# Sixteen PSUM copies given to ScalarE and four weight tiles converted one place later, in a fused attention and feed-forward kernel

## The chip, the cores and the metric

The kernel runs on one core of a Trainium2 chip. The metric is the time of one execution on the device in microseconds, the median of several runs. The engines are named as in the profile: PE is TensorE's matmuls, PEld its weight loads, DVE is VectorE, ACT is ScalarE, POOL is GpSimd and SP issues the loads.

## What is computed

Causal attention with 2 batches, 12 heads, 448 positions and 64 columns per head gives x of 896 x 768. Then come two feed-forward blocks:

```python
x = attention(q, k, v)                       # 896 x 768
y = ((x @ w1) * (x @ w2)) @ w3 @ w_out       # w1, w2: 768 x 1024; w3: 1024 x 1024; w_out: 1024 x 768
z = np.maximum(y @ w_in2, 0) ** 2 @ w_out2   # w_in2: 768 x 2048; w_out2: 2048 x 768
```

The weights arrive as 8-byte floats, so a tile is loaded as pairs of 32-bit words, and float32 is made of them in the kernel.

## The kernel before

The kernel multiplies w3 by w_out first, while the attention runs, into W (the SBUF tile `wraw`), so that the first block ends in one product with W. This product is cut into 32 **units** (g, i, n): half g of the 1024 inner columns, row tile i of eight, half n of the 768 output columns. A unit is a chain of matmuls into one accumulator of 384 columns (`w_half`, called by `fill`), 12 matmuls in two-part float32 (8 plain float32 ones for the first two row tiles), and one eviction behind it: in the half g = 0 a copy from PSUM into `wraw` (L318), in the half g = 1 an addition onto it (L316). The 16 units with g = 0 come first.

The attention runs over 12 pairs of heads in 13 **slots**. In slot p TensorE computes the scores of pair p, transposes the probabilities of pair p-1 (`p_transposes`, L273), and multiplies them by v (`attend`). In between stand three fills, which place two or three units in a slot from slot 2 on; from slot 4 on the order on TensorE is scores, unit, transposes, units, attend. VectorE takes the row minima of the scores (`minima`, L238), ScalarE the exponentials (`exps`, L245, one call for each head j of a pair) and copies the transposed probabilities out of PSUM (L277), GpSimd divides by the row sums (L255; VectorE does so for a few), and ScalarE and VectorE make the high and the low part of the attended columns (`x_parts`, L119 and L120).

The same two engines convert the weights, in calls of `step`. A step takes one tile from 8-byte words to float32 (the prelu of L102 on ScalarE, L103 and L108 on VectorE) and the tile before it to a high and a low part (the cast of L90 on ScalarE, the subtraction of L106 on VectorE). Which tiles they are follows from the list `order`. A step leaves the float32 part out if two converted tiles still wait for their parts, and leaves the parts out if the buffer is not free; the parts of w3 tile n wait for the units of tile n-2. Each step also issues the loads on SP (L78) of tiles three places ahead.

On TensorE, VectorE and ScalarE the order of this stage is the order in which the code calls the operations (`manual_schedule`, L363). Each engine works through its queue in that order, and an instruction that waits holds up those behind it. So in slot p, from slot 4 on, ScalarE does the exps of head 0, the copies of the transposes, a step, the exps of head 1, further steps and the high part of the attend before; VectorE does the minima, the copy of the first unit, a step, after the exps of head 1 the copies of the other units, further steps and the low part of the attend. Slots 2 and 3 differ in the place of the third unit, which comes behind the attend.

Two pools of PSUM buffers set the waits between the engines. `ps_w` has two: the accumulators of the units and of `attend` take them in turn, so each waits for the eviction of the last but one. Unit (0,1,0) waits for the copy of (0,0,1), unit (0,2,1) for that of (0,2,0), the attend of pair 4 for that of (0,5,0), the attend of pair 5 for that of (0,6,1). `ps_a` has six: the transposes of slot p take the six that the scores of slot p were in, so they wait for the minima of slot p; the next scores wait for ScalarE's copies of these transposes.

After slot 12 the big products follow, x by w1 and w2, by W, by w_in2 and by w_out2, whose order a planner sets.

Of the kernel before, what the change touches and what calls it, by code (L numbers as in the profile page):

```python
# [17 lines left out]
def attention_moe_moe2(ctx: ExitStack, tc: tile.TileContext, qk, v, w1, w2, w3, w_out, w_in2, w_out2, out):  # L18
# [13 lines left out]
    nc = tc.nc  # L32
# [35 lines left out]
    def mm(o, l, r, start, stop):  # L68
        return nc.tensor.matmul(o, l, r, start=start, stop=stop)  # L69
# [61 lines left out]
    NB = W3N // P  # L131
    order = []
    for g in range(N3 // KF):
        for i in range(KF):
            order += [("w3", g * KF + i)]
            if g == 0 and i == 0:
                order += [("wout", f) for f in range(NB)]
            if g == 0 and NB - 1 <= i < 2 * NB - 1:
                order += [("wout", i + 1)]
    order += ring[KF:]  # L140
    source = {"wout": w_out, "w1": w1, "w2": w2, "w3": w3, "win2": w_in2, "wout2": w_out2}
    place = {key: i for i, key in enumerate(order)}
# [36 lines left out]
    with (  # L179
# [121 lines left out]
        def w_half(g, i, n):  # L301

            n3, cols = g * KF + i, slice(n * HN, (n + 1) * HN)
            acc = ps_w.tile([P, HN], F32, tag="w", name=f"w{n3}_{n}")
            for f in range(NB):
                c = slice(f * P, (f + 1) * P)
                if n3 < PLAIN:
                    mm(acc, f32s["w3", n3][:, c], f32s["wout", f][:, cols], f == 0, f == NB - 1)
                    continue
                t, wo = hls["w3", n3], hls["wout", g * NB + f]  # L310
                for s, r in ((0, 0), (0, 1), (1, 0)):
                    mm(acc, t[:, s, c], wo[:, r, cols],
                       f == 0 and (s, r) == (0, 0), f == NB - 1 and (s, r) == (1, 0))
            dst = wraw[:, i, cols]
            if g > 0:
                nc.vector.tensor_tensor(dst, acc, dst, op=ALU.add)  # L316
            else:
                nc.vector.tensor_copy(dst, acc)  # L318

        units = [(g, i, n) for g in range(N3 // KF) for i in range(KF) for n in range(2)]  # L320
        NU = len(units)
# [33 lines left out]
        def fill():  # L355
            done[0] += 1
            n = max(0, done[0] - LEAD) * NU // (GAPS * SLOTS - LEAD) - done[1]
            for _ in range(n):
                w_half(*units.pop(0))
                done[1] += 1  # L360
# [159 lines left out]
    acc = big.tile([P, NTT, DM], F32, tag="W", name="acc")  # L520
# [92 lines left out]
```

## Time and profile before

| | us |
|---|---|
| median of 3 runs | 577.47 |
| lowest and highest run | 577.46, 577.71 |
| the profiled execution | 577.6 |
| its span, from the first to the last instruction | 575.4 |
| PE busy in the span | 563.9 |
| DVE busy | 281.3 |
| ACT busy | 268.2 |
| POOL busy | 159.1 |

A busy time is the sum over an engine's instructions. The chain that ended last is followed back from the last instruction, at each step to what released it. In a timeline the first number is the start in us from the span's start, the second the time from the first start to the last end of a run of equal instructions, and the bracket at the end is the idle time before the row and what ended it. An instruction's end overlaps the start of the next one on the same engine.

### The profile page before, as it was taken

To read this page: it belongs to the slowest core of one execution; us is meant where nothing else is said; L and a number is where in the kernel's file an instruction comes from. 1 tells how busy PE (TensorE), PEld (TensorE's weight loads), DVE (VectorE), ACT (ScalarE), POOL (GpSimd) and SP (SyncE) were. 2 spreads that over 40 slices of the span, in tenths; PEclk is the share of its full clock that TensorE was granted. 3 is DMA by queue.
4 is the path that set the end of the run, shared out by engine and by line. 5 is a ranking of instruction groups with operands and counts; after the bars stand their busy time and mean duration, and the time that the engine had idled before them with its cause. 6 is when DMAs were issued, how large, how long until landed. Compare 5 with 4: busy or idle time off the path is not lost.

```text
span 575.4 us, 8129 instructions
## 1 busy us (share of the span) xinstructions
PE 563.9 (98%) x3144; PEld 506.5 (88%) x3144; DVE 281.3 (49%) x567; ACT 268.2 (47%) x574; POOL 159.1 (28%) x140
## 2 busy tenths in 40 slices
PE   7899999999999999999999999999999999999997
PEld 5557777778989999999999999999999999999997
DVE  5987887767687544222210484555102854421011
ACT  5778777757865533222210456666002666640000
POOL 3367677776200312111100003333000023330000
PEclk9999999999999999999999999999999999999999
DMA  8854554233266633000000274333100763000111
GB/s 318 288 194 140 177 159 159 84 124 120 88 225 245 204 120 107 9 1 1 1 1 0 67 271 156 109 111 110 56 1 4 270 219 110 1 1 29 56 55 56
DMA packets 14823, 63.96 MB, mean 111 GB/s; under 512 B 1665, under 2 KB 1921, under 8 KB 14785
## 3 DMA queue, kind: packets, MB, share of 16 engines
q1 hardware_dynamic: 14784, 63.45, 32.2%
q8 instruction: 25, 0.41, 0.3%
q14 instruction: 14, 0.11, 0.1%
HBM read 60.69 MB, written 2.75 MB: 110 GB/s over the span
## 4 chain that ended last, share of the span: by engine, by line
PE 86%; DVE 6%; ACT 5%; issue 1%; DMA 1%; DVEq 0%; ACTq 0%
PE w L69 28%; PE g L69 20%; PE o L69 20%; PE h L69 10%; PE s L69 3%; PE x L69 2%; PE pp L273 2%; ACT p L245 2%; ACT pt L277 2%; DVE p L238 1%; DVE xw L108 1%; DMA qk<-in_qk 1%; ACT hl_wout L90 1%; DVE raw_wout L103 0%; DVE x_wout L108 0%
## 5 line engine op out<-in xcount | busy, mean ns | idle before, releaser
L69 PE MATMUL g<-hT,hl_win 128*128 128x448 f32 x576 | 117.2, 365 | 0.0
L69 PE MATMUL w<-xT,hl_w 128*128 128x448 f32 x576 | 117.0, 365 | 0.0
L69 PE MATMUL o<-hl_wout,gT 128*128 128x384 f32 x672 | 116.9, 334 | 0.0
L69 PEld LDWEIGHTS o<-hl_wout,gT 128*128 128x128 f32 x672 | 116.6, 188 | 0.1
L69 PEld LDWEIGHTS g<-hT,hl_win 128*128 128x128 f32 x576 | 108.1, 188 | 8.5
L69 PEld LDWEIGHTS w<-xT,hl_w 128*128 128x128 f32 x576 | 108.1, 188 | 8.5
L255 POOL TENSOR_SCALAR p<-p,st 112x448 f32<-112x448 f32 (+1 forms) x84 | 96.5, 1166 | 51.9 <-DVE st L252 23.3
L120 POOL TENSOR_TENSOR gT<-r,gT 128x448 fp32r<-128x448 f32 x32 | 39.1, 1245 | 195.8 <-ACT gT L119 128.7
L69 PE MATMUL w<-hl_wout,w 128*128 128x384 f32 x336 | 64.4, 342 | 0.5 <-DVE w L106 0.3
L245 ACT ACTIVATE p<-p,st 112x448 f32<-112x448 f32 (+1 forms) x96 | 49.7, 530 | 27.1 <-DVE st L238 27.0
L69 PEld LDWEIGHTS w<-hl_wout,w 128*128 128x128 f32 x336 | 57.4, 188 | 3.9 <-issue 0.9
L69 PE MATMUL h<-abT,hl_W 128*128 128x448 f32 x288 | 58.5, 365 | 0.0
L69 PEld LDWEIGHTS h<-abT,hl_W 128*128 128x128 f32 x288 | 54.1, 188 | 4.3
L120 POOL TENSOR_TENSOR abT<-a,abT 128x448 fp32r<-128x448 f32 x16 | 21.8, 1377 | 111.8 <-ACT abT L119 111.8
L238 DVE CUSTOM_DVE_ANT_0 p<-s,mask 112x448 f32<-112x448 f32 (+1 forms) x96 | 36.5, 441 | 7.0 <-PE s L69 7.0
L106 DVE TENSOR_TENSOR hl_wout<-x_wout,hl_wout 128x768 fp32r<-128x768 f32 x20 | 19.1, 957 | 37.9 <-ACT hl_wout L90 37.9
L533 ACT ACTIVATE r<-g 128x448 f32<-128x448 f32 x32 | 15.8, 542 | 40.8 <-PE g L69 40.8
L69 PE MATMUL s<-qk 64*112 64x448 f32 (+3 forms) x192 | 28.6, 443 | 4.1 <-DMA qk<-in_qk 4.1
L560 DVE TENSOR_TENSOR acc<-o,acc 128x384 f32<-128x384 f32 x14 | 7.2, 553 | 49.0 <-PE o L69 49.0
L273 PE MATMUL pp<-ident,p 112*112 112x112 f32 x240 | 27.9, 262 | 3.3 <-DVE st L238 1.6
L102 ACT ACTIVATE x_w<-raw_w 128x768 f32<-128x768 f32 (+1 forms) x30 | 24.4, 815 | 13.7 <-DVE hl_w L106 10.9
L273 PEld LDWEIGHTS pp<-ident,p 112*112 112x112 f32 x240 | 23.5, 134 | 8.0 <-issue 2.8
(62 smaller groups left out, 538.0 us busy)
## 6 DMA issues: line engine op xcount, KB each, us to landing
raw_wout<-in_w_out SPq DMA_DIRECT2D x24, 768.0 KB, 4.5
raw_w<-in_w SPq DMA_DIRECT2D x16, 768.0 KB, 4.3
raw_win<-in_w_in SPq DMA_DIRECT2D x16, 768.0 KB, 4.2
raw_w<-in_w SPq DMA_DIRECT2D x16, 512.0 KB, 3.9
qk<-in_qk SPq DMA_DIRECT2D x12, 448.0 KB, 5.1
v<-in_v SPq DMA_DIRECT2D x12, 224.0 KB, 2.6
out<-acc SPq DMA_DIRECT2D x6, 384.0 KB, 2.3
out<-acc SPq DMA_DIRECT2D x2, 192.0 KB, 1.8
```

The source lines that it names most:

```text
L69: return nc.tensor.matmul(o, l, r, start=start, stop=stop)
L90: nc.scalar.copy(t[:, 0], x)
L102: nc.scalar.activation(y, high.bitcast(F32), AF.Prelu, scale=2.0 ** -112, alpha=-2.0 ** 32)
L106: nc.vector.tensor_tensor(t[:, 1], x, t[:, 0].bitcast(F32), op=ALU.subtract)
L120: (engine or nc.vector).tensor_tensor(lo, x, hi.bitcast(F32), op=ALU.subtract)
L238: nc.vector.tensor_tensor_reduce(e, ps[j, i], mask[:, S - (i + 1) * CP:], QS, 3.0e38, ALU.add, ALU.min, st_t[p][:, 0, j, i:i + 1],)
L245: nc.scalar.activation(e, e, AF.Exp, bias=st_t[p][:, 0, j, i:i + 1], scale=-1.0, accum_out=st_t[p][:, 1, j, i:i + 1])
L255: engine.tensor_scalar(e, e, st[:, 3, i:i + 1], None, ALU.mult)
L273: nc.tensor.transpose(x[:CP, o:o + CP], pt[:, off[i] + c * CP:off[i] + (c + 1) * CP], ident[:CP, :CP],)
L277: nc.scalar.copy(t[:, coff[g[0]]:coff[g[0]] + o], x[:CP, :o])
L533: nc.scalar.activation(r, o[b], AF.Relu)
L560: nc.vector.tensor_tensor(a, o[n], a, op=ALU.add)
```

## The change

In the first half (g = 0) the copy of a unit's accumulator to `wraw` is made by ScalarE and not by VectorE; the call stays at its place in `w_half`, so it lies in ScalarE's queue where it lay in VectorE's. In the list `order`, tiles 4 to 7 of w_out move one place of w3 down: they stood behind w3 tiles 3 to 6, and stand behind w3 tiles 4 to 7.

```diff
             order += [("w3", g * KF + i)]
             if g == 0 and i == 0:
                 order += [("wout", f) for f in range(NB)]
-            if g == 0 and NB - 1 <= i < 2 * NB - 1:
-                order += [("wout", i + 1)]
+            if g == 0 and NB <= i < 2 * NB:
+                order += [("wout", i)]
     order += ring[KF:]
...
             if g > 0:
                 nc.vector.tensor_tensor(dst, acc, dst, op=ALU.add)
             else:
-                nc.vector.tensor_copy(dst, acc)
+                nc.scalar.copy(dst, acc)
```

Here NB is 4 and KF is 8. With the rules of `step` the new order gives these steps where they differ: in slot 2 the loads of w3 4 and w_out 4, and of w3 5 and w_out 5, change places. In slot 3 the second step makes the float32 of w3 4 (it was w_out 4), the last one that of w_out 4 alone (it was w3 4, and the parts of w_out 4). In slot 4 the first step makes the parts of w3 4 alone (it also made the float32 of w_out 5); the parts of w_out 4 to 7 follow in the second step of slot 4, the first and the last of slot 5, and the second of slot 6, and their float32 part comes in the step before each. The first step of slot 7 also makes the float32 of w3 10. Each w3 tile gets its parts in the same step as before.

## Rows read from the trace of the kernel before

**Rows 1.** Windows: PE, PEld, DVE, ACT, POOL busy (count), PEclk, DMA share, GB/s.

```profile
22.00:92.00 70.00, 66.33 (x408) 47.53 (x406) 58.09 (x169) 52.42 (x144) 47.55 (x40) 1.00 0.52 164
92.00:575.00 483.00, 480.07 (x2618) 446.19 (x2616) 208.79 (x349) 199.73 (x387) 102.39 (x87) 1.00 0.27 93
```

**Rows 2.** Timeline of PE: start, us, operation, count, idle before and its releaser.

```profile
33.58 2.85 PE L69 MATMUL w<-xw,w 128*128 128x384 f32 x8 [0.20 <-DVE wraw L318]
...
41.12 2.81 PE L273 MATMUL pp<-ident,p 112*112 112x112 f32 x20
43.70 2.35 PE L69 MATMUL w<-hl_wout,w 128*128 128x384 f32 x12
...
48.31 2.36 PE L69 MATMUL w<-hl_wout,w 128*128 128x384 f32 x12 [0.23 <-DVE wraw L318]
...
54.89 2.08 PE L273 MATMUL pp<-ident,p 112*112 112x112 f32 x20
...
75.04 2.11 PE L69 MATMUL x<-pt,v 112*64 112x448 f32 x16
...
88.03 2.03 PE L69 MATMUL w<-hl_wout,w 128*128 128x384 f32 x10 [0.30 <-DVE w L106]
89.99 2.11 PE L69 MATMUL x<-pt,v 112*64 112x448 f32 x16
...
98.14 2.34 PE L69 MATMUL w<-hl_wout,w 128*128 128x384 f32 x12
...
108.57 4.42 PE L69 MATMUL w<-hl_wout,w 128*128 128x384 f32 x24
...
119.23 2.08 PE L273 MATMUL pp<-ident,p 112*112 112x112 f32 x20
```

**Rows 3.** Groups by line and form: busy us, mean ns | idle before, releasers.

```profile
L318 DVE COPY wraw<-w 128x384 f32<-128x384 f32 x16 | 8.7, 547 | 0.0
...
L556 ACT COPY acc<-o 128x384 f32<-128x384 f32 x7 | 3.4, 479 | 35.3 <-PE o L69 35.3
...
L102 ACT ACTIVATE x_wout<-raw_wout 128x768 f32<-128x768 f32 x20 | 18.3, 917 | 5.6 <-DVE hl_win L106 3.7 <-DMA raw_wout<-in_w_out 1.9
...
L102 ACT ACTIVATE x_w<-raw_w 128x512 f32<-128x512 f32 x14 | 9.7, 695 | 1.4 <-DVE w L106 1.4
```

**Rows 4.** Timeline of ACT; four rows follow directly on exps of head 1.

```profile
33.99 0.83 ACT L90 CAST hl_wout<-xw 128x768 fp32r<-128x768 f32 x1
...
48.60 0.54 ACT L119 CAST xT<-x 128x448 fp32r<-128x448 f32 x1
...
75.37 0.62 ACT L90 CAST w<-x_w 128x512 fp32r<-128x512 f32 x1
...
84.24 2.29 ACT L277 COPY pt<-pp 112x448 f32<-112x448 f32 x6
...
89.55 0.61 ACT L90 CAST w<-x_w 128x512 fp32r<-128x512 f32 x1
```

**Rows 5.** Timeline of DVE: a copy, first minima of slots 5 to 8, what follows.

```profile
32.97 0.55 DVE L318 COPY wraw<-w 128x384 f32<-128x384 f32 x1
...
67.13 0.61 DVE L238 CUSTOM_DVE_ANT_0 p<-s,mask 112x448 f32<-112x448 f32 x1
...
81.52 0.61 DVE L238 CUSTOM_DVE_ANT_0 p<-s,mask 112x448 f32<-112x448 f32 x1
...
94.22 0.62 DVE L238 CUSTOM_DVE_ANT_0 p<-s,mask 112x448 f32<-112x448 f32 x1
...
104.68 0.61 DVE L238 CUSTOM_DVE_ANT_0 p<-s,mask 112x448 f32<-112x448 f32 x1
...
107.63 0.55 DVE L316 TENSOR_TENSOR wraw<-w,wraw 128x384 f32<-128x384 f32 x1
```

**Rows 6.** DMA issues on the page: count, KB each, median us to landing.

```profile
raw_wout<-in_w_out SPq DMA_DIRECT2D x24, 768.0 KB, 4.5
```

**Rows 7.** The chain that ended last, in order of time: start, us, what.

```profile
61.59 0.44 DVE wraw L318
```

## The prediction

> **What bounds the kernel now.** I read the busy windows first, then TensorE's timeline, then what VectorE and ScalarE do just before each gap in it, last the chain that ended last. From 92 us on TensorE lacks 2.93 of 483 us, which is the last tile's way out behind its last matmul; before that it lacks 3.67 of 70 us, though VectorE is busy for 58.1 of them and ScalarE for 52.4 [rows 1]. So whatever TensorE loses or wins before about 110 us moves the end by as much, if nothing before the full stretch gives it back. The granted clock is 1.00 in both windows, 2.4 GHz, so it is no part of the sum.
>
> The gaps are of three kinds [rows 2]. A unit or an attend waits for its ps_w buffer: 0.20 us at 33.58 and 0.23 at 48.31, both released by the copies of L318. The transposes wait for the row minima of their own slot, which free the six ps_a banks: such a group of twenty takes 2.81 us (41.12; three others are alike, at 25.93, 67.90 and 82.29) instead of 2.08 (54.89). A unit waits for the low part of its w3 tile: 0.30 at 88.03. The reader should see that ps_w has two buffers, so that TensorE may be no more than one eviction ahead, and that every one of these waits ends within 0.1 us of what VectorE has just done. The sixteen copies never waited for TensorE: no idle time stands before them [rows 3].
>
> **The copies.** On VectorE each costs 547 ns, on ScalarE a copy of the same 128x384 from PSUM costs 479 [rows 3]. Instructions overlap their successor: six pt copies of 2,240 columns together take 2.29 us from first start to last end (84.24) [rows 4], 0.39 for 384 columns, and the last one's end still overlaps; I put a copy at 0.37 us of queue time. Bounds: nothing, where ScalarE would idle anyway, and 0.48, without overlap. What matters is where it stands in ScalarE's written order: the first unit's copy of a slot comes behind exps(p,0) and ahead of the pt copies, the others behind exps(p,1) and ahead of the conversions. VectorE now copies in parallel with exps(p,1): at 32.97 [rows 5], 0.5 us before that block of exponentials ends (33.99) [rows 4]. On ScalarE the same copy must let the block end first. Queued behind a copy are the pt copies, the conversions, exps(p,1) and the attention casts; TensorE waits for all of them.
>
> **The order of tiles.** Every w3 tile gets its high and low part in the same step as now, tiles 4 to 7 of w_out one step with a free place later. Written out step by step: slot 3's last step makes only the f32 of w_out 4, slot 4's first only the parts of w3 4, slot 6's middle step also the parts of w_out 7, and slot 7's first also the f32 of w3 10; from then on all is as before. An f32 of w_out instead of w3 costs ScalarE 0.22 us more (917 against 695 ns) [rows 3]; dropping one in slot 4 saves 0.8 (its 0.92 less the overlap), the extra one in slot 7 costs 0.57 in the same way. On SP the loads of w_out trade places with those of w3 only, and keep their places among the loads of q, k and v; they stay ahead of their use by over 10 us, against 4.5 us to land [rows 6], and the first user of w_out 4 to 7 is slot 7's second unit, some 5 us behind the last conversion: both at nothing. With that cover gone the unit would wait for one step, about 2 us.
>
> **The sum, slot by slot** (times now, then shifts; a release costs some 0.06 us).
> Slot 2: exps(2,1) ends at 33.99, plus 0.37 for the copy ahead of it, so the copy of unit (0,0,1) ends at 34.36 + 0.48 = 34.84 instead of 33.52, and unit (0,1,0) starts 1.3 us late.
> Slot 3: ScalarE is 0.74 late, VectorE saves a copy of 0.47 on the way to the minima: they come 0.27 late, and transposes paced by them would end at 43.97. TensorE reaches the transposes at 41.12 + 1.3 = 42.4 and is through unstretched at 42.4 + 1.9 = 44.3; unit (0,2,0) starts at 43.70 now, so +0.6 is left. exps(3,1) end at 48.60 + 0.27 + 0.37 - 0.22 = 49.0; copy of (0,2,0) until 49.5; unit (0,2,1) at 49.5 against 48.31: **+1.2**.
> Slot 4: the transposes at 54.89 were not waiting, so the +1.2 stays. ScalarE's pt copies follow the transposes (+1.15), the missing f32 gives 0.8 back, two copies take 0.74, of which VectorE saves 0.44 on the chain [rows 7], and one of them waits about 0.1 for TensorE: minima of slot 5 at +0.75, 67.9 against 67.13 [rows 5].
> Slot 5: eight minima take 2.95 us (104.68 to 107.63) [rows 5] and the last three transposes 0.35 more (three twentieths of 2.08 and a release): the next unit at 71.2, as late as the minima, +0.75. exps(5,1) end at 75.37 + 0.75 + 0.37 = 76.5, the copy of (0,5,0) at 76.97, so attend(4) starts at 77.05 against 75.04: **+2.0**. The way to the minima of slot 6 now runs over ScalarE, late by 1.12 and two copies, and saves VectorE's two copies of 0.44: 82.5 against 81.52.
> Slot 6: the transposes are paced by the minima, +1.0. The cast of w3 7 comes 1.0 + 0.37 later, so does the unit that waited at 88.03: 89.4. exps(6,1) end at 89.55 + 1.0 + 0.37 + 0.22 = 91.2; copy of (0,6,1) 91.65; attend(5) at 91.7 against 89.99: **+1.7**.
> Slot 7: with two copies and w_out 7's parts in one queue (copies to 91.9, cast 92.65, low part 93.6, f32 and low part of w3 8 95.5, f32 of w3 9 and attend's low part) the minima start at 96.65 and their transposes end 3.3 later at 99.95; arriving late, at 98.0 plus 1.9, TensorE says the same. The first unit behind them starts at 98.14 now: **+1.8**.
> Slot 8: from the minima of slot 7 to those of slot 8 ScalarE has a copy (0.37) and the extra f32 (0.57) more, so they start at 104.68 + 2.43 + 0.94 = 108.05, where 2.43 is how late slot 7's are (94.22 now [rows 5]); the last of them and its transposes end at 111.35 against 108.57: **+2.8**.
> Slot 9 on: transposes reach TensorE at 121.9 (119.23 + 2.7), behind minima that start at 119.6; TensorE is the last again and keeps **+2.8 us**.
> From there TensorE is full to the end, so the span goes from 575.4 to 578.2; the profiled execution took 577.6, the median of the runs is 577.47, and I predict 580.3. The copies alone, without the changed order, come to some 2.2 in the same manner, since slots 7 and 8 keep their slack.
>
> **Rivals.** *VectorE's relief wins.* VectorE is the busier engine up to 92 us [rows 1], and four of its copies lie on the chain that ended last with 0.44 to 0.48 us each, one shown [rows 7]. If ScalarE's share fits into its waits for the minima, these 1.8 us are won: 575.7. It decides if the copy of the second unit doesn't hold up TensorE. Against it: those waits come ahead of exps(p,0), the copies behind. The Trainium skill, Perfetto Trace Analysis, Optimizing Scalar/DVE Operations, says that an overloaded DVE may hand work to Scalar, and gives DVE about 125 ns overhead on PSUM against 51 on Scalar. By that rule this rival would be the forecast; the trace agrees on the cheaper copy (479 against 547) and not on what it leads to, since the rule looks at the load and not at the place in the queue.
> *Stretch absorbs it.* Four groups of transposes are stretched by 0.74 us, 3.0 in all [rows 2]; if minima come no later than now, late units only eat that stretch, and not more than 1.1 us is left: 577.5 to 578.6. Against it: the second gap of each pair (48.31, 75.04, 89.99) lies behind the stretch.
> *More is lost.* At 0.48 us of queue time for each of some 13 copies on ScalarE's path, 1.4 us come on top: 581.7. The same happens if GpSimd's division of slot 7, which starts later with exps(7,1), holds up slot 8.
> *The copies move elsewhere in the queue* and cost nothing: the trace of before follows the written order of the three engines in this stage, so I give it no chance of its own.
>
> **How the numbers follow.** Forecast (about +2.8, from 1.2 to 3.6) 0.66, more is lost 0.14, stretch absorbs it 0.12, VectorE's relief 0.08. A measurement of this kernel can tell about 0.2%, 1.15 us, from no change; the third case lies within it, the first two above. Slower 0.80, same 0.12, faster 0.08. The range leaves out, below, relief and nearly all of the third case, and above, the part of the second that is over 582.0: 578.5 to 582.0.
>
> **What would show it.** Right: TensorE's waits at unit (0,1,0), unit (0,2,1), attend(4) and attend(5) are released by ScalarE's copy and last 0.4 to 1.7 us; the minima of slots 7 and 8 start 2 to 4 us later than now; from about 112 us on all is shifted by one amount. Wrong: those waits stay near 0.2 us, or the shift shrinks again behind slot 6, because the copy's place costs less than the end of exps(p,1) says.

## The result and the profile after

The changed kernel takes 581.14 us (median of 5 runs, 581.05 to 581.35) against 577.65 of the kernel before on the same chip: a ratio of 1.0062, 95% interval 1.0048 to 1.0076, so 3.5 us slower (2.8 to 4.4). The span of the profiled execution grew from 575.4 to 578.9 us.

The same two windows as in [rows 1], of the changed kernel (us; busy PE, PEld, DVE, ACT, POOL with counts; PEclk, DMA share, GB/s):

```profile
22.00:92.00 70.00, 63.75 (x392) 46.34 (x390) 46.69 (x147) 55.16 (x153) 46.69 (x38) 1.00 0.45 148
92.00:575.00 483.00, 482.54 (x2630) 447.02 (x2631) 210.25 (x354) 203.46 (x394) 105.27 (x88) 1.00 0.28 95
```

VectorE got what it was to get: 46.69 us busy instead of 58.09. Of the difference some 8 us are the copies; most of the rest is work that now falls behind 92 us. ScalarE took 2.7 us more, and TensorE lacks 6.25 us of this window instead of 3.67. Some 1.2 us more are lost behind it, in slots 7 and 8, where the transposes take 2.34 and 2.82 us and not 2.08.

TensorE's timeline, for [rows 2] (start, us, operation, count, idle before with its releaser):

```profile
34.84 2.85 PE L69 MATMUL w<-xw,w 128*128 128x384 f32 x8 [1.53 <-ACT wraw L318]
...
42.38 2.08 PE L273 MATMUL pp<-ident,p 112*112 112x112 f32 x20
44.23 2.34 PE L69 MATMUL w<-hl_wout,w 128*128 128x384 f32 x12
...
49.40 2.37 PE L69 MATMUL w<-hl_wout,w 128*128 128x384 f32 x12 [0.79 <-ACT wraw L318]
...
77.53 2.11 PE L69 MATMUL x<-pt,v 112*64 112x448 f32 x16 [1.42 <-ACT wraw L318]
...
92.32 2.11 PE L69 MATMUL x<-pt,v 112*64 112x448 f32 x16 [0.48 <-ACT wraw L318]
...
98.66 2.34 PE L273 MATMUL pp<-ident,p 112*112 112x112 f32 x20
100.77 2.35 PE L69 MATMUL w<-hl_wout,w 128*128 128x384 f32 x12
...
109.50 2.82 PE L273 MATMUL pp<-ident,p 112*112 112x112 f32 x20
112.08 4.41 PE L69 MATMUL w<-hl_wout,w 128*128 128x384 f32 x24
...
122.73 2.08 PE L273 MATMUL pp<-ident,p 112*112 112x112 f32 x20
```

Four waits for an accumulator buffer stand there, of 1.53, 0.79, 1.42 and 0.48 us, each released by a ScalarE copy; before, VectorE's copies made it wait 0.20 and 0.23 [rows 2]. The last row starts 3.50 us behind its fellow of before (119.23), and this is what the median lost: nothing behind slot 9 gives any of it back.

Some pieces of the chain that ended last (start, us, what); [rows 7] has one of the four copies of VectorE that stood in it before:

```profile
28.39 0.46 ACT wraw L318
...
34.43 0.36 ACT wraw L318
...
48.98 0.38 ACT wraw L318
...
62.34 0.02 ACT wraw L318
...
77.11 0.75 ACT wraw L318 x2
...
91.90 0.38 ACT wraw L318
```

Before, four copies on VectorE were links of this chain, of 0.44 to 0.48 us each, 1.8 in all. Now ScalarE's copies are links in slots 2, 3, 5 and 6, with 3.4 us in all. In slot 4 the chain runs through TensorE, and the copy has 0.02 us of it.

### The profile page after: what moved, and what is told of

The parts are those of the page before. It is cut to its first block, busy times and chain, and to the rows that moved or that the text cites. A ratio compares the mean times of both kernels' runs of the same rounds, so it can differ in the third digit from the quotient of the medians.

```text
span 578.9 us, 8132 instructions
## 1 busy us (share of the span) xinstructions
PE 564.3 (97%) x3144; PEld 506.2 (87%) x3144; DVE 272.0 (47%) x551; ACT 274.8 (47%) x590; POOL 161.1 (28%) x140
## 4 chain that ended last, share of the span: by engine, by line
PE 86%; ACT 7%; DVE 5%; issue 1%; DMA 1%; DVEq 0%
PE w L69 28%; PE g L69 20%; PE o L69 20%; PE h L69 10%; PE s L69 3%; ACT p L245 3%; PE pp L273 2%; PE x L69 2%; ACT pt L277 1%; DVE p L238 1%; DVE xw L108 1%; ACT hl_wout L90 1%; ACT wraw L318 1%; DMA qk<-in_qk 1%; ACT x_wout L102 0%
## 5 line engine op out<-in xcount | busy, mean ns | idle before, releaser
L255 POOL TENSOR_SCALAR p<-p,st 112x448 f32<-112x448 f32 (+1 forms) x84 | 98.9, 1194 | 53.0 <-DVE st L252 23.8
L69 PE MATMUL s<-qk 64*112 64x112 f32 (+3 forms) x192 | 28.5, 437 | 4.1 <-DMA qk<-in_qk 4.0
```

Source lines behind the costliest of these rows:

```text
L255: engine.tensor_scalar(e, e, st[:, 3, i:i + 1], None, ALU.mult)
```

## The experiments

All times are medians beside runs of the kernel before on the same chip (577.50 us in each of the two series). The edits are shown against the changed kernel, and that of the last run against the kernel before. Two theories run through them. **Place**: a copy costs what its position in ScalarE's queue holds up, TensorE's next accumulator above all. **Load**: each copy costs alike, because ScalarE has more to do.

### The copies alone

```diff
-            if g == 0 and NB <= i < 2 * NB:
-                order += [("wout", i)]
+            if g == 0 and NB - 1 <= i < 2 * NB - 1:
+                order += [("wout", i + 1)]
```

> The sixteen copies are on ScalarE, the order of tiles is that of before. Place (the copies cost by what waits behind them in ScalarE's queue, above all TensorE's four waits for its accumulator buffer): 2.2 us slower than before, 579.8, and unit (0,1,0) starts 1.3 us later than in the kernel before; about 1.3 us of the change's 3.5 are then the order's. Copies are everything: 3.5 us slower, 581.1, and the order costs nothing. VectorE's relief: not slower than before.

Measured: 579.33 us, ratio 1.0035 (1.0022 to 1.0047), by the ratio 2.0 us slower. Unit (0,1,0) waits 1.5 us, as in the full change. From slot 9 on TensorE runs 2.1 us behind the kernel before (scores of slot 9 at 117.06 against 114.96). The copies are the larger part, and VectorE's relief does not outweigh them.

### The order alone

```diff
-                nc.scalar.copy(dst, acc)
+                nc.vector.tensor_copy(dst, acc)
```

> The copies are back on VectorE, the order of tiles is the changed one. Place: TensorE's waits for its accumulator buffers are those of before (0.2 us at units (0,1,0) and (0,2,1)); the f32 of w3 10 in slot 7 and the parts of w_out 7 in slot 6 delay the minima of slots 7 and 8 by 0.5 to 1 us, of which 0.6 us is left: 578.2. The order costs nothing by itself: 577.6, within 0.3 us of before. If the two parts simply add, this run and that of the copies alone give 3.5 us together.

Measured: 577.95 us, ratio 1.0008 (1.0000 to 1.0017), about 0.45 us slower, at the edge of what can be told from no change. That lies between the two expectations. The wait at unit (0,2,1) is gone, which had been expected to stay. The trace shows a gain and a larger loss: attend(5) starts 0.9 us ahead of the kernel before (89.11 against 89.99), then the minima pace the transposes of slots 7 and 8, which take 2.08 us each in the kernel before.

```profile
89.11 2.11 PE L69 MATMUL x<-pt,v 112*64 112x448 f32 x16
...
95.42 2.68 PE L273 MATMUL pp<-ident,p 112*112 112x112 f32 x20
...
106.46 2.55 PE L273 MATMUL pp<-ident,p 112*112 112x112 f32 x20
...
119.44 2.08 PE L273 MATMUL pp<-ident,p 112*112 112x112 f32 x20
```

By slot 9 TensorE is 0.2 us behind (119.44 against 119.23). The two parts give 2.4 us one by one and 3.5 together: they do not add. The same places with the copies alone:

```profile
92.09 2.11 PE L69 MATMUL x<-pt,v 112*64 112x448 f32 x16 [0.21 <-ACT wraw L318]
...
108.82 2.08 PE L273 MATMUL pp<-ident,p 112*112 112x112 f32 x20
...
121.33 2.08 PE L273 MATMUL pp<-ident,p 112*112 112x112 f32 x20
```

Four traces side by side show where the sum fails (start in us; up to 0.2 us of a difference between two traces stands already ahead of slot 2's copies):

| TensorE's work | before | order alone | copies alone | both |
|---|---|---|---|---|
| attend(1), slot 2 | 31.27 | 31.12 | 31.10 | 31.21 |
| attend(5), slot 6 | 89.99 | 89.11 | 92.09 | 92.32 |
| transposes of slot 9 | 119.23 | 119.44 | 121.33 | 122.73 |

From attend(5) to slot 9 the order costs 1.1 us alone (30.33 against 29.24) and 1.2 beside the copies (30.41 against 29.24); the copies cost nothing there. So the later loss adds up, and no slack in slots 7 and 8 is spent twice. What does not add is the order's early gain: from attend(1) to attend(5) it is 0.7 us alone (57.99 against 58.72), and beside the copies it is a loss of 0.1 (61.11 against 60.99). One row of the changed kernel and two of the copies alone show what became of it:

```profile
52.85 0.62 DVE L238 CUSTOM_DVE_ANT_0 p<-s,mask 112x448 f32<-112x448 f32 x1 [0.88 <-PE s L69]
```

```profile
62.25 0.88 ACT L318 COPY wraw<-w 128x384 f32<-128x384 f32 x2
62.98 0.88 ACT L90 CAST hl_wout<-x_wout 128x768 fp32r<-128x768 f32 x1
```

With less to convert in slot 3, VectorE is ready early for the minima of slot 4, but it waits 0.88 us for the scores of TensorE, which the copies have made late (0.59 with the copies alone). In slot 4 ScalarE begins its copies 0.9 us earlier than with the copies alone (61.35 against 62.25); the second one must wait for TensorE's unit until 62.34, so the cast behind it gains only 0.27 (62.71 against 62.98).

### Four copies, and the other twelve

```diff
-            else:
+            elif (i, n) in ((0, 1), (2, 0), (5, 0), (6, 1)):
                 nc.scalar.copy(dst, acc)
+            else:
+                nc.vector.tensor_copy(dst, acc)
```

The second kernel has `not in` in place of `in`. Both have the changed order.

> The changed order; only the copies of units (0,0,1), (0,2,0), (0,5,0) and (0,6,1), whose buffer TensorE takes next, are on ScalarE, the other twelve on VectorE. Place: these four carry most of the loss, 2.0 us slower than before, 579.6. Load (each copy on ScalarE costs alike, a sixteenth of the loss that is not the order's): 0.7 us for four copies and 0.6 for the order, 578.9.

> The changed order; the copies of units (0,0,1), (0,2,0), (0,5,0) and (0,6,1) are on VectorE, the other twelve on ScalarE. Place: TensorE's waits of over 0.3 us for an accumulator buffer go, and the rest of the loss is what the first copy of a slot adds ahead of the exponentials: 1.5 us slower than before, 579.1, less than with the four alone. Load: twelve sixteenths of 2.9 us and 0.6 for the order, 2.8 us slower, 580.4, more than with the four alone.

Measured: with the four 578.91 us, ratio 1.0023 (1.0014 to 1.0032), 1.4 us slower; with the twelve 578.74, ratio 1.0022 (1.0013 to 1.0031), 1.2 us slower. Less the order's 0.45, the four cost about as much as the twelve. The first run alone does not decide: 1.4 lies close to the 1.3 that load wanted, and place wanted 2.0. The second does, for load wanted 2.8. TensorE's waits, first with the four, then with the twelve on ScalarE (us in total, times, longest):

```profile
PE w L69 <- ACT wraw L318: 2.0, 2, 1.1
PE x L69 <- ACT wraw L318: 1.0, 1, 1.0
```

```profile
PE w L69 <- DVE wraw L320: 0.6, 1, 0.6
PE x L69 <- ACT p L245: 0.5, 1, 0.5
```

Four copies bring 3.0 us of waits for them, twelve others none. But with the twelve TensorE does not run free, as had been expected: it waits 0.6 us for VectorE's copy of (0,0,1), and 0.55 us at attend(4). The profile puts the second wait down to an exponential; VectorE's copy of (0,5,0), whose buffer attend(4) takes, ends 0.1 us ahead of it:

```profile
73.87 0.54 DVE L320 COPY wraw<-w 128x384 f32<-128x384 f32 x1
```

```profile
74.52 2.11 PE L69 MATMUL x<-pt,v 112*64 112x448 f32 x16 [0.55 <-ACT p L245]
```

Both times came out 0.3 to 0.6 us under what place had promised. Nor do these two halves add: beside the order they cost some 0.95 and 0.8 us, and all sixteen copies 3.0.

### The second copy ahead of the exponentials

```diff
-                    exps(p, 1)
                     fill()
+                    exps(p, 1)
                     divide(p, 1)
```

The same exchange is made in slots 2 and 3.

> The whole change, and the second unit of a slot stands ahead of the exponentials of head 1 in the written order, so that ScalarE copies it before exps(p,1) and not behind; TensorE's and VectorE's work is the same. Place: unit (0,1,0) starts when it did in the kernel before or up to 0.5 us earlier (33.1 to 33.6), attend(4) waits under 0.5 us, and of the loss of 3.5 us some 2.2 are left, 579.8. If only ScalarE's load counted, nothing would change: 581.1.

Measured: 579.89 us, ratio 1.0043 (1.0029 to 1.0057), 2.4 us slower, so 1.1 us of the loss are gone (1.25 by the medians themselves) although ScalarE does the same work. ScalarE's queue in slot 2 of this kernel, and TensorE's unit (0,1,0) and transposes of slot 6:

```profile
32.20 0.51 ACT L318 COPY wraw<-w 128x384 f32<-128x384 f32 x1
32.56 0.72 ACT L245 ACTIVATE p<-p,st 112x448 f32<-112x448 f32 x1
```

```profile
33.21 2.85 PE L69 MATMUL w<-xw,w 128*128 128x384 f32 x8
...
82.57 2.82 PE L273 MATMUL pp<-ident,p 112*112 112x112 f32 x20 [1.38 <-POOL p L255]
```

The copy is made 2.1 us earlier than in the changed kernel (34.31 there) and the unit no longer waits. The waits for accumulator buffers are gone in the whole trace. From attend(1) to attend(5) this wins 1.8 us over the changed kernel (31.18 to 90.44, 59.26 against 61.11); slots 7 and 8 take 0.5 of it back, where the transposes take 2.82 us each. In slot 6 part of the gain has turned into another wait: the exponentials are a copy later, so GpSimd divides later, and the transposes wait 1.38 us for it, against 0.77 in the kernel before:

```profile
82.29 2.82 PE L273 MATMUL pp<-ident,p 112*112 112x112 f32 x20 [0.77 <-POOL p L255]
```

### Each copy made twice

```diff
                 nc.scalar.copy(dst, acc)
+                nc.scalar.copy(dst, acc)
```

> The whole change with each of the sixteen copies made twice by ScalarE, the second over the first, 0.36 us of queue time more for each. Place, with nearly every copy of a slot on the path from minima to minima while ScalarE is the last there: some 12 of the 16 count, 4.5 us more than with the change, 585.6. If only the four waits of TensorE for its buffers counted, 1.4 us more: 582.5.

Measured: 588.80 us, ratio 1.0197 (1.0183 to 1.0212), 7.7 us over the changed kernel, more than either had expected. Two things had been left out. The first is the size of a second copy:

```profile
34.65 0.50 ACT L318 COPY wraw<-w 128x384 f32<-128x384 f32 x1
35.19 0.48 ACT L319 COPY wraw<-w 128x384 f32<-128x384 f32 x1
35.56 0.83 ACT L90 CAST hl_wout<-xw 128x768 fp32r<-128x768 f32 x1
```

From one copy to its repetition 0.54 us pass, from the repetition to the cast 0.37. Over the sixteen pairs the first distance is 0.48 to 0.55 us, 0.52 in the mean. Each repetition starts just behind the end of the copy ahead, and the cast does not. The repetition reads and writes what the copy did; which of the two makes it wait no run separates.

The second is TensorE's clock. Unit (0,1,0) of this kernel, and the stretch 38 to 40 us (busy PE, PEld, DVE, ACT, POOL with counts; PEclk, DMA share, GB/s):

```profile
35.72 4.34 PE L69 MATMUL w<-xw,w 128*128 128x384 f32 x8 [2.54 <-ACT wraw L319]
```

```profile
38.00:40.00 2.00, 2.00 (x6) 0.61 (x4) 1.97 (x5) 0.86 (x2) 1.52 (x2) 0.50 0.51 91
```

TensorE sat idle for 2.54 us ahead of this unit, and in it the granted clock fell to 0.50, the level of 1.2 GHz. The unit takes 4.34 us and not 2.85. In the changed kernel, behind a wait of 1.53 us, the clock stays at 1.00. Behind another wait of 2.38 us, later in this kernel, it stays there too, so these rows do not show what decides.

Sixteen times 0.52 are 8.3 us. Of the 7.7 that arrived, the clock has some 1.5, an estimate from the two lengths of the unit. That leaves 6.2 us, or 12 of the 16 copies, the number expected.

### The f32 of w3 10 out of slot 7's first step

```diff
                     p_transposes(2 * (p - 1) + 1)
-                    step()
+                    step(f32=p != 7)
```

> The whole change, but the first step of slot 7 makes only the parts of w3 9; the f32 of w3 10 comes one step later. If the f32 that the order brings to slot 7 is what makes slot 8 long: minima of slot 8 start 0.5 us earlier than in the changed kernel, TensorE begins the first unit behind them 0.5 us earlier, and 0.2 to 0.5 us of the 3.5 are given back, 580.7. If it is something else, the start of the minima of slot 8 stays within 0.2 us of 108.7.

Measured: 580.58 us, ratio 1.0054 (1.0041 to 1.0067), 0.56 us less than the change by the medians and 0.4 beside the kernel before, the intervals of the two overlapping. The trace is the clearer witness. The first of the minima of slot 8, and the transposes that they pace:

```profile
107.70 0.62 DVE L238 CUSTOM_DVE_ANT_0 p<-s,mask 112x448 f32<-112x448 f32 x1
```

```profile
108.92 2.39 PE L273 MATMUL pp<-ident,p 112*112 112x112 f32 x20
```

Against 108.73 and 2.82 in the changed kernel. This trace is 0.4 us ahead already at the minima of slot 7 (96.99 against 97.41), so 0.6 of the 1.0 us are the edit's. From the minima of slot 7 to those of slot 8 there are 10.71 us and not 11.32; with the copies alone there are 10.72. The extra f32 is what makes slot 8 long. Some 0.2 us of this is lost again in slot 9, whose transposes take 2.28 us.

### Two copies only, the order of before

```diff
-            else:
+            elif (i, n) in ((1, 0), (5, 1)):
+                nc.scalar.copy(dst, acc)
+            else:
                 nc.vector.tensor_copy(dst, acc)
```

> The order of before; only the copies of units (0,1,0) and (0,5,1) are on ScalarE, the others on VectorE. These two close the VectorE queue of slots 2 and 5 just ahead of the next minima, nothing of TensorE's waits for them soon, and ScalarE is idle or ahead there. Place: 0.9 us faster than before, 576.6, the minima of slots 3 and 6 start 0.4 to 0.6 us earlier. Load (each copy on ScalarE costs a sixteenth): 0.2 us slower, within what can be told from no change.

Measured: 576.68 us, ratio 0.9986 (0.9977 to 0.9995), 0.8 us faster than before and 4.5 faster than the change. The copy of (0,1,0) on ScalarE, and VectorE's first minima of slots 3 and 6:

```profile
36.99 0.52 ACT L318 COPY wraw<-w 128x384 f32<-128x384 f32 x1
```

```profile
39.72 0.61 DVE L238 CUSTOM_DVE_ANT_0 p<-s,mask 112x448 f32<-112x448 f32 x1
...
80.55 0.61 DVE L238 CUSTOM_DVE_ANT_0 p<-s,mask 112x448 f32<-112x448 f32 x1
```

In the kernel before these stand at 40.34 and at 81.52, the second in [rows 5]. The first copy brings some 0.5 us, the second 0.35 more; this trace starts 0.15 us ahead. Behind the first copy and the cast that follows it ScalarE still waits 2.3 us for the next minima, and VectorE's queue is shorter just where the minima wait in it. Sixteen copies moved lose 2.0 us, these two win 0.8.

## Why the prediction was right, and where it was short

The forecast was 580.3, slower by 2.8; measured are 581.14 and 3.5. The mechanism is the one forecast, and the first three steps of the sum fall within 0.1 us of the trace: unit (0,1,0) at 34.9 (34.84), unit (0,2,0) at 44.3 (44.23), unit (0,2,1) at 49.5 (49.40). The stretch of slot 3's transposes did absorb over half of the first loss: they take 2.08 us instead of 2.81, and of 1.26 us 0.53 are left.

**The term that was mis-sized is slot 4's.** The minima of slot 5 were put at 67.9 and start at 68.34, 1.2 us later than before and not 0.75. Two rows of the changed kernel say why, one of ScalarE and one of VectorE:

```profile
62.34 0.48 ACT L318 COPY wraw<-w 128x384 f32<-128x384 f32 x1 [0.48 <-PE w L69]
```

```profile
63.58 1.25 DVE L106 TENSOR_TENSOR hl_wout<-x_wout,hl_wout 128x768 fp32r<-128x768 f32 x1 [1.36 <-ACT hl_wout L90]
```

The sum took back 0.8 us for the f32 that slot 4's first step leaves out. But ScalarE's second copy of the slot waits 0.48 us for TensorE's unit, where the sum had 0.1, and holds the cast of w_out 4 behind it; the low part then takes 1.25 us, where its fellows take 0.96. Little of the 0.8 is left: TensorE, late by 1.1 us from slot 3, was what ended last here. From there on every forecast runs 0.5 to 0.8 us early, with nearly the right steps in between: attend(4) at 77.05 (77.53), minima of slot 6 at 82.5 (83.12), attend(5) at 91.7 (92.32), minima of slot 7 at 96.65 (97.41), the unit behind slot 7's transposes at 99.95 (100.77), minima of slot 8 at 108.05 (108.73), the next unit at 111.35 (112.08), the transposes of slot 9 at 121.9 (122.73).

**The queue time of a copy**, put at 0.37 us, is 0.35 (34.31 to the cast at 34.66 in the changed kernel), and 0.35 to 0.38 where another copy's successor did not wait; the rows of the sixteen have a mean of 487 ns. The bound of 0.48 was not needed. So the rival that more is lost came nearer with its 581.7 than the forecast did, but by luck, for neither of its causes shows in the rows. Its second one, GpSimd's division, is named by the profile in slot 8 (PEld is TensorE's loading of weights, here for the transposes):

```profile
106.57 4.06 POOL L255 TENSOR_SCALAR p<-p,st 112x448 f32<-112x448 f32 x4 [0.74 <-ACT x_w L102]
```

```profile
110.75 0.08 DVE L238 DVE_READ_ACCUMULATOR2_ANT st<- 112x1 f32 x1
...
110.94 0.67 PEld L273 LDWEIGHTS pp<-ident,p 112*112 112x112 f32 x7 [0.32 <-POOL p L255]
```

The division ends at 110.63, and VectorE's minimum, whose bank these transposes take, at 110.83. By these rows VectorE was the last; the profile's times for GpSimd are rough, and no run separates the two.

**The split** was nearly right for the copies (2.2 forecast, 2.0 measured), and slots 7 and 8 did keep their slack with the copies alone. But the order's share is not a fixed 0.6: it is 0.45 alone and about 1.5 on top of the copies. Its loss in slots 7 and 8 is the same in both; its early gain falls away beside the copies, the 0.8 of slot 4 included.

**VectorE's relief**, the rival on the other side, and the advice of the Trainium skill (Perfetto Trace Analysis, Optimizing Scalar/DVE Operations) that an overloaded DVE may hand work over: the trace bears out that the copy is cheaper on ScalarE (487 against 547 ns). For sixteen copies the result speaks against it, for two it holds, with 0.8 us. What decides is what stands behind the copy in the queue, as the exchange with the exponentials shows with the load unchanged.

**Stretch absorbs it** fell as argued: it took up part of the first loss, and the second wait of each pair lies behind the stretch. Of the order's loads and of w_out's late tiles nothing showed; TensorE waited for none of them.

What stays open: the sums for four and for twelve copies came out 0.6 and 0.3 us too high, the first just outside its interval and the second inside, and why these two halves cost 1.75 us beside the order and the sixteen together 3.0 was not followed up. The exchange with the exponentials shows the place for 1.1 us of the loss; for the rest of the copies' share it is read from the traces.

## What to carry to other kernels

Before work is moved from a busy engine to a less busy one, look at where it lands in the other queue: behind which instruction it must wait, and who waits for its result. Here a PSUM copy that ran beside a block of exponentials came to stand behind it, and with two accumulator buffers TensorE paid for much of the wait. Look for the pieces that end the busy engine's queue just ahead of what everyone waits for, and that nobody waits for soon; here two such copies won 0.8 us, where sixteen lost 2.0. And measure two changes together as well as one by one: a gain of one is worth nothing where the other has made a different engine the late one.

## What the runs showed of the hardware

On ScalarE a copy of 128x384 float32 from PSUM holds the queue for 0.35 to 0.38 us, though its row says some 0.48, when the next instruction works on other data; when the next one is the same copy again, 0.48 to 0.55 us pass. The reader of a profile should take queue time from start to start, and ask whether neighbours touch the same data. And an experiment that adds work can change the clock: behind 2.54 us of idle time TensorE ran part of a unit at a granted clock of 0.50, which had to be taken out of the sum.
